# One unit instead of two on plain products, and the order of the first steps, in a fused recurrence-and-MLP kernel

**Chip, cores, metric.** One core of one Trainium2 chip. The metric is the device time of one execution in microseconds (us), median of several executions. The kernel before takes 569.28 us (568.92 to 569.32, three runs). Engine names are those of the profile: PE is TensorE, PEld its weight loads, DVE VectorE, ACT ScalarE, POOL GpSimd.

## The reference

A gated linear recurrence over 768 tokens (4 batches, 8 heads of 48), whose outputs are the 3072 x 384 input of an MLP with an ELU between its two products:

```python
f = 1.0 / (1.0 + np.exp(-f_logit))
for t in range(S):
    state = f[:, :, t, :, None] * state + np.einsum('bhd,bhe->bhde', k[:, :, t], v[:, :, t])
    y[:, :, t] = np.einsum('bhd,bhde->bhe', q[:, :, t], state)
...
h = x @ w_in                                    # 3072x384 @ 384x2048
g = np.where(h > 0.0, h, np.exp(np.minimum(h, 0.0)) - 1.0)
return (g @ w_out).astype(np.float32)           # 3072x2048 @ 2048x384
```

## The kernel before

The 3072 tokens are worked off in twelve **units** of 256. A unit's MLP is eight **pairs**; a pair is one **up** step (part of `x @ w_in`) and, two pairs later, one **down** step (part of `g @ w_out`). Counting ups and downs alike gives steps T0, T1, ...; sixteen belong to a unit. Everything else (attention of the next units, weights, loads) is hung onto steps with `at_step(T, ...)`.

A step has two forms. The *direct* form is plain block products. The *seven-product* form (Strassen-like, 2x2 blocks in seven products) has less PE work and more additions. Units with `m < DIRECT` use the direct form:

```python
DIRECT = 2                      # units 0 and 1 are direct
A1 = (2, 4, 4, 5, 7, 9)         # steps of unit 1's attention; the last three: scores and masks, outputs, carried
D2 = (14, 16, 18, 20); A2 = (22, 24, 24, 26, 27, 28)
MX = 21                         # first mix of the in-weights (POOL)
...
both = (0, 1, 2, 3, 4, 5, 8, 9, 10, 6, 11, 7, 12, 13, 14, 15)    # pairs of units 0 and 1, interleaved
order = [divmod(i, NP) for i in both] + [(m, j) for m in range(2, NU) for j in range(NP)]
...
def down(P):
    m, j = order[P]
    if j == 0:
        pms[m] = [ps.tile([128, DM], FP32, tag=f"m{i + 2 * (m == 1)}", ...) for i in range(NW if m < DIRECT else 4)]
```

The weights arrive as 64-bit numbers in staging slots `area[:, 0..6]`, in sixteen parts, and each part is turned into 32-bit by three steps on two engines: DVE *splits*, ACT *lowers*, DVE *merges*. Seven parts may be under way; a merge frees a slot and fetches the next part:

```python
def split(n):
    nc.vector.tensor_scalar(out=bits[:], in0=hi, scalar1=3, scalar2=0x3FFFFFF8, ...)      # L559
    nc.vector.tensor_scalar(out=hi, in0=hi, scalar1=-(2**30), ...)                        # L563
def lower(n):
    nc.scalar.activation(raw.bitcast(U16)[:, 2::4], raw.bitcast(U32)[:, 0::2], AF.Copy, ...)   # L569
def merge(n):
    nc.vector.tensor_tensor(out=to.bitcast(I32), in0=bits, in1=hi, op=ALU.add)            # L577
    fetch(n + AHEAD)
...
combos = area[:, 0:4]...        # differences of out-weights for the seven products (DVE, `combine`)
mixes = area[:, 4:7]...         # sums of in-weights for the seven products (POOL, `mix`)
...
attention(1, (), A1)
for n in range(1, NFT):
    t = max(needs[n][0] - 2, 0)
    at_step(t, lambda n=n: merge(n))
    if n > 1:
        later.setdefault(max(t - 2, 0), []).append(n)        # split and lower, two steps earlier
at_step(4, lambda: load(2))
at_step(12, lambda: gates(2))
```

## Time and profile before

| | before |
|---|---|
| median of 3 runs | 569.28 us |
| span of the profiled run | 567.4 us |
| first up step, T0 | 29.25 us |
| attention outputs of unit 1 | 51.34 us |
| up step T16 | 77.08 us |
| up step T32 (unit 2 begins) | 124.46 us |
| up step T48 (unit 3 begins) | 168.81 us |

All positions are starts on PE, counted from the beginning of the span, in the timeline of PE. The lines of the page, the chain, the start and the groups are in the prediction below.

### The profile page before, as it was taken

The page shows a single profiled execution, that of the slowest core. Times are in us where ns is not written, and L with a number is a line of the kernel's source. Part 1 is how long each engine was busy: PE and PEld are TensorE (multiplying, and loading weights), DVE is VectorE, ACT ScalarE, POOL GpSimd, SP SyncE. Part 2 cuts the span into 40 slices and gives each one's busy share as a digit, 9 for nine tenths or more (in the row PEclk, how much of TensorE's full clock was granted, in tenths as well). Part 3 has the DMA queues.
Part 4 walks back from the last instruction along what each step waited for, and adds up shares of the span by engine and source line. Part 5 has one row for each costly group of instructions (what it writes and reads, how often), then busy time and mean ns, then how long its engine had stood idle before and what let it go on. Part 6 is the DMA issues. An engine that isn't in the chain of part 4 may idle for free.

```text
span 567.4 us, 15202 instructions
## 1 busy us (share of the span) xinstructions
PE 550.2 (97%) x6226; PEld 501.8 (88%) x6226; DVE 395.2 (70%) x765; ACT 229.3 (40%) x417; POOL 266.3 (47%) x530
## 2 busy tenths in 40 slices
PE   6879999999999999999999999999999999999996
PEld 3457777778999999999999999999999999999995
DVE  8798485835976795885785885786786876745543
ACT  3297737334343443434333343343333343333331
POOL 6510027642374474465366357257257348325332
PEclk9998999999999999999999999999999999999999
DMA  8989780060025125215216216216206203201001
GB/s 207 259 215 297 174 223 14 2 161 29 2 50 140 58 60 143 73 45 152 79 36 155 85 37 154 84 38 154 84 20 172 84 9 72 85 2 36 29 2 35
DMA packets 37902, 53.27 MB, mean 94 GB/s; under 512 B 3680, under 2 KB 27648, under 8 KB 37824
## 3 DMA queue, kind: packets, MB, share of 16 engines
q1 hardware_dynamic: 37024, 51.62, 34.6%
q8 instruction: 51, 0.84, 0.6%
q10 hardware_dynamic: 800, 0.59, 0.5%
q14 instruction: 27, 0.22, 0.1%
HBM read 44.04 MB, written 4.72 MB: 86 GB/s over the span
## 4 chain that ended last, share of the span: by engine, by line
PE 92%; DVE 3%; DMA 2%; issue 1%; ACT 1%; POOL 1%; SPq 0%; DVEq 0%; ACTq 0%; POOLq 0%
PE psH L878 35%; PE psM L977 33%; PE psM L955 8%; PE psH L923 6%; PE psS L701 2%; PE psY L739 2%; PE psY L759 2%; PE psU_a L724 2%; PE psT L665 2%; DMA f<-f 1%; DVE f L627 1%; DMA f<-in_f_logit_dram 1%; ACT area L569 1%; DVE bits L559 0%; PE psY L804 0%
## 5 line engine op out<-in xcount | busy, mean ns | idle before, releaser
L878 PE MATMUL psH<-xt,wi 128*128 128x128 f32 (+1 forms) x960 | 177.1, 293 | 0.0
L942 POOL TENSOR_TENSOR sums<-gg 128x128 f32<-128x128 f32 x160 | 69.5, 455 | 210.8 <-DVE gg L932 202.5
L878 PEld LDWEIGHTS psH<-xt,wi 128*128 128x128 f32 x960 | 135.9, 192 | 0.8
L910 ACT ACTIVATE gg<-hh 128x512 f32<-128x512 f32 x80 | 50.5, 631 | 205.9 <-DVE hh L900 140.5
L878 PE MATMUL psH<-xt,area 128*128 128x128 f32 x640 | 110.5, 275 | 0.0
L878 PEld LDWEIGHTS psH<-xt,area 128*128 128x128 f32 x640 | 96.9, 192 | 4.1
L887 DVE TENSOR_TENSOR hh<-psH,u 128x256 f32<-128x256 f32 x80 | 33.8, 423 | 88.7 <-ACT u L885 88.7
L977 PE MATMUL psM<-area,sums 128*128 128x192 f32 x480 | 91.2, 326 | 0.0
L977 PEld LDWEIGHTS psM<-area,sums 128*128 128x128 f32 x480 | 80.1, 190 | 0.2 <-POOL sums L942 0.2
L977 PE MATMUL psM<-wo,gg 128*128 128x192 f32 x320 | 68.1, 335 | 0.0
L617 POOL TENSOR_TENSOR k<-k,f 128x256 f32<-128x256 f32 x48 | 39.4, 822 | 57.1 <-DMA area<-in_moe_w_in_dram 35.0
L627 DVE RECIPROCAL f<-f 128x256 f32<-128x256 f32 x36 | 62.8, 1747 | 1.3
L911 ACT ACTIVATE gg<-gg 128x512 f32<-128x512 f32 x96 | 60.6, 631 | 3.0
L932 DVE SCALAR_TENSOR_TENSOR gg<-gg,hh 128x512 f32<-128x512 f32 x80 | 55.7, 696 | 1.8 <-ACT gg L911 1.8
L977 PEld LDWEIGHTS psM<-wo,gg 128*128 128x128 f32 x320 | 50.2, 190 | 1.9
L900 DVE TENSOR_TENSOR hh<-psH,u43h 128x256 f32<-128x256 f32 (+1 forms) x160 | 49.8, 353 | 2.7
L923 PE MATMUL psH<-xt,wi 128*128 128x256 f32 x192 | 44.5, 381 | 1.4 <-DVE wi L577 1.2
L942 POOL TENSOR_TENSOR sums<-gg,sums 128x128 f32<-128x128 f32 x80 | 42.8, 535 | 6.3
L955 PE MATMUL psM<-wo,gg 128*128 128x384 f32 x128 | 45.4, 498 | 0.0
L885 ACT COPY u<-psH 128x128 f32<-128x128 f32 x80 | 21.0, 263 | 59.3 <-PE psH L878 59.3
L923 PEld LDWEIGHTS psH<-xt,wi 128*128 128x128 f32 x192 | 35.9, 190 | 8.6 <-issue 1.6
L900 DVE TENSOR_TENSOR u43h<-psH,hh 128x256 f32<-128x256 f32 x80 | 33.9, 423 | 13.4 <-PE psH L878 13.0
(97 smaller groups left out, 721.9 us busy)
## 6 DMA issues: line engine op xcount, KB each, us to landing
area<-in_moe_w_out_dram SPq DMA_DIRECT2D x8, 768.0 KB, 8.9
again<-in_moe_w_in_dram SPq DMA_DIRECT2D x16, 384.0 KB, 4.1
again<-in_moe_w_out_dram SPq DMA_DIRECT2D x16, 384.0 KB, 3.5
k<-in_k_dram SPq DMA_DIRECT2D x12, 384.0 KB, 4.8
q<-in_q_dram SPq DMA_DIRECT2D x12, 384.0 KB, 5.5
v<-in_v_dram SPq DMA_DIRECT2D x12, 384.0 KB, 5.9
area<-in_moe_w_in_dram SPq DMA_DIRECT2D x8, 576.0 KB, 7.2
out_dram<-o SPq DMA_DIRECT2D x38, 96.0 KB, 1.7
```

Source lines behind the costliest of these rows:

```text
L617: e.tensor_tensor(out=t[n][:, p], in0=t[n][:, p], in1=t["f"][:, p, "kq".index(n)], op=ALU.mult)
L627: nc.vector.reciprocal(f[:, p, 1], f[:, p, 0])
L878: nc.tensor.matmul(to, lhsT=lhs, rhs=rhs, start=(n == 0), stop=True, skip_group_check=True)
L887: add = lambda to, x, y: nc.vector.tensor_tensor(out=to, in0=x, in1=y, op=ALU.add)
L900: add = lambda to, x, y: nc.vector.tensor_tensor(out=to, in0=x, in1=y, op=ALU.add)
L910: nc.scalar.activation(g[:], h, AF.Relu, scale=-1.0)
L911: nc.scalar.activation(g[:], g[:], AF.Exp, scale=-1.0)
L923: nc.tensor.matmul(ph[:, i], lhsT=wi[j][:, kt, i * 128 : (i + 1) * 128], rhs=xts[m][:, kt, :], start=(kt == 0), stop=(kt == NKT - 1),)
L932: nc.vector.scalar_tensor_tensor(out=g[:], in0=g[:], scalar=-1.0, in1=phs.pop(P), op0=ALU.add, op1=ALU.max)
L942: nc.gpsimd.tensor_tensor(out=s[:, i], in0=x, in1=y, op=op)
L955: nc.tensor.matmul(pm[t][:], lhsT=g[:, i, t * 128 : (t + 1) * 128], rhs=wo[:, 2 * j + i, :], start=(j == 0 and i == 0), stop=(j == NP - 1 ...
L977: nc.tensor.matmul(pm[bank][:, half * DH : (half + 1) * DH], lhsT=x, rhs=y, start=first, stop=(j == NP - 1), skip_group_check=True,)
```

## The change

The intent: unit 1 too takes the seven-product form, so unit 0 runs its MLP alone while the weights come in, in plain order. The mixes and combinations then have to be ready sooner; they are made in the staging slots as these come free (slots 2 to 4 for the mixes, 5, 6, 0, 1 for the combinations). The first steps are arranged anew: unit 1's state additions at T5, scores at T7, outputs at T8, carried states at T9, and each merge no later than step n.

```diff
-    DIRECT = 2
+    DIRECT = 1
...
-    A1 = (2, 4, 4, 5, 7, 9)
-    D2 = (14, 16, 18, 20)
-    A2 = (22, 24, 24, 26, 27, 28)
+    A1 = (2, 4, 5, 7, 8, 9)
+    D2 = (16, 18, 20, 22)
+    A2 = (23, 25, 25, 26, 27, 28)
...
-    MX = 21
+    MX = 10
+    CB = 16
+    BL1 = 13
...
+        combos = [area[:, i].bitcast(FP32).rearrange("p (n f) -> p n f", f=DH) for i in (5, 6, 0, 1)]
...
-        area[:, 4:7].bitcast(FP32).rearrange("p a f -> p (a f)")[:, 0 : NP * 512]
+        area[:, 2:5].bitcast(FP32).rearrange("p a f -> p (a f)")[:, 0 : NP * 512]
...
-    both = (0, 1, 2, 3, 4, 5, 8, 9, 10, 6, 11, 7, 12, 13, 14, 15)
-    order = [divmod(i, NP) for i in both] + [(m, j) for m in range(2, NU) for j in range(NP)]
+    order = [divmod(i, NP) for i in range(NU * NP)]
...
-            ... tag=f"m{i + 2 * (m == 1)}" ...
+            ... tag=f"m{i + (m < DIRECT)}" ...
...
-        t = max(needs[n][0] - 2, 0)
+        t = min(max(needs[n][0] - 2, 0), n)
...
-    at_step(4, lambda: load(2))
-    at_step(12, lambda: gates(2))
+    at_step(8, lambda: load(2))
+    at_step(14, lambda: gates(2))
...
-        at_step(28 + n, lambda: next(weights))
+        at_step(CB + n, lambda: next(weights))
...
+    at_step(BL1, lambda: blend(1))
```

More of the change, by code (lines that the diff above doesn't have):

```diff
@@ L509, in fast @@
     area = cst.tile([128, AHEAD, 2 * DM], w_in.dtype, name="area") if wide else None
-    combos = cst.tile([128, 4, NP, DH], FP32, name="combos") if not wide else (
-        area[:, 0:4].bitcast(FP32).rearrange("p a f -> p (a f)").rearrange("p (c n f) -> p c n f", c=4, f=DH)
-    )
+    if wide:
+        combos = [area[:, i].bitcast(FP32).rearrange("p (n f) -> p n f", f=DH) for i in (5, 6, 0, 1)]
+    else:
+        apart = cst.tile([128, 4, NP, DH], FP32, name="combos")
+        combos = [apart[:, i] for i in range(4)]
     mixes = cst.tile([128, NP, 4, 128], FP32, name="mixes") if not wide else (
-        area[:, 4:7].bitcast(FP32).rearrange("p a f -> p (a f)")[:, 0 : NP * 512]
+        area[:, 2:5].bitcast(FP32).rearrange("p a f -> p (a f)")[:, 0 : NP * 512]
         .rearrange("p (n c f) -> p n c f", n=NP, c=4)
     )
-    both = (0, 1, 2, 3, 4, 5, 8, 9, 10, 6, 11, 7, 12, 13, 14, 15)
-    order = [divmod(i, NP) for i in both] + [(m, j) for m in range(2, NU) for j in range(NP)]
+    order = [divmod(i, NP) for i in range(NU * NP)]
     needs = sorted(
@@ L840, in combine @@
         b = [[wo[:, i::2, h * DH : (h + 1) * DH] for h in range(2)] for i in range(2)]
-        t = [combos[:, i] for i in range(4)]
+        t = combos
         for n in range(0, NP, 2):
@@ L948, in down @@
         if j == 0:
-            pms[m] = [ps.tile([128, DM], FP32, tag=f"m{i + 2 * (m == 1)}", name=f"psM{m}_{i}") for i in range(NW if m < DIRECT else 4)]
+            pms[m] = [ps.tile([128, DM], FP32, tag=f"m{i + (m < DIRECT)}", name=f"psM{m}_{i}") for i in range(NW if m < DIRECT else 4)]
         pm, g = pms[m], gs.pop(P)
@@ L969, in down @@
         b = [[wo[:, 2 * j + i, h * DH : (h + 1) * DH] for h in range(2)] for i in range(2)]
-        c = [combos[:, i, j] for i in range(4)]
+        c = [combos[i][:, j] for i in range(4)]
         for bank, half, x, y in (
```

## The prediction

> **What bounds the kernel now.** I read the page first: busy shares, then the 40 slices.
>
> ```profile
> PE 550.2 (97%) x6226; PEld 501.8 (88%) x6226; DVE 395.2 (70%) x765; ACT 229.3 (40%) x417; POOL 266.3 (47%) x530
> PE   6879999999999999999999999999999999999996
> DVE  8798485835976795885785885786786876745543
> ```
>
> TensorE (PE) is full from the fifth slice on; only the first four (57 us) have room, and there VectorE (DVE) is nearly full. Next the chain of work that ended last: from 48.8 us on it is PE work almost alone, so PE time saved there is span saved, if nothing else takes its place. It also gives the price of each kind of MLP step (columns: start, us, what).
>
> ```profile
> 43.29 1.72 PE psS L701 x62
> 45.01 3.81 PE psM L955 x8
> 48.82 2.59 PE psH L923 x12
> ...
> 116.88 2.58 PE psM L955 x8
> 119.46 2.59 PE psH L923 x12
> ...
> 164.25 2.44 PE psH L878 x20
> 166.69 2.28 PE psM L977 x14
> ```
>
> A direct pair (six up products L923, four down products L955) takes 2.59 + 2.58 = 5.17 us. A seven-product pair (L878, L977) takes 2.44 + 2.28 = 4.72 us. Then the timeline of PE at the start, and the windows there (after the colon: length; busy us of PE, PEld, DVE, ACT, POOL with counts; clock, DMA share, GB/s).
>
> ```profile
> 37.35 2.83 PE L923 MATMUL psH<-xt,wi 128*128 128x256 f32 x12 [0.19 <-PE psU_a L724]
> 42.78 0.29 PE L701 MATMUL psS<-q,k 64*64 64x64 f32 x2 [2.60 <-issue]
> 43.29 1.72 PE L701 MATMUL psS<-q,k 64*64 64x64 f32 x62 [0.21 <-DVE state L682]
> 44.94 3.88 PE L955 MATMUL psM<-wo,gg 128*128 128x384 f32 x8
> ...
> 44.00:48.00 4.00, 4.00 (x43) 2.59 (x36) 3.90 (x7) 1.93 (x1) 0.00 (x0) 0.62 1.05 251
> ```
>
> PE stands 2.6 us before the scores (L701). They reuse the banks that the four state additions (L682) still read, and DVE reaches these only at 41.4. The clock then drops to 0.62, and the first down step takes 3.81 us, not 2.58. Last the groups, for the weight conversion and the other side work.
>
> ```profile
> L627 DVE RECIPROCAL f<-f 128x256 f32<-128x256 f32 x36 | 62.8, 1747 | 1.3
> L569 ACT ACTIVATE area<-area 128x768 uint16<-128x768 uint32 x16 | 30.4, 1934 | 4.1 <-DVE area L563 3.2 <-DMA q<-in_q_dram 0.8
> L622 DVE TENSOR_TENSOR_SCAN f<-f 128x256 f32<-128x256 f32 x36 | 26.6, 746 | 1.0 <-ACT f L610 1.0
> L577 DVE CUSTOM_DVE_ANT_0 wi<-area,bits 128x1536 uint16<-128x1536 uint16 x8 | 8.0, 1001 | 4.2 <-ACT area L569 3.8 <-ACT between L746 0.4
> L846 DVE TENSOR_TENSOR area<-wo,area 128x384 f32<-128x384 f32 x8 | 5.6, 702 | 0.0
> ```
>
> Each of 16 weight parts costs about 1.15 us of DVE (split, L559 and L563), 1.93 us of ScalarE (ACT, L569), and 1.0 us of DVE (merge, L577).
>
> **What the Trainium skill says.** "Perfetto Trace Analysis", its opening note, calls matmul busy time a bad measure, as matmuls are pipelined. The trace agrees: L878 shows 293 ns for one instruction, but 20 of them take 2.44 us, 122 ns each; so I price steps from the chain. "TensorE: Matmul & The Clock Gate", section "Architectural detail", says ACT and DVE are strict FIFO while PE can pull weight loads ahead. It agrees: unit 0's third up step ended at 40.2, but its activation began at 42.55, behind two L569 passes. Same page, "What's actually happening": the clock halves after an idle window of about 3.4 us. That fits the 0.62 above, after a stretch of 40 to 44 us in which PE was busy 1.19 us. "ScalarE: Activation LUTs", "What ACT_TABLE_LOAD costs", gives 186 + 0.833 N ns for an ACTIVATE with immediates: 613 ns at 512 columns, where the trace has 608 to 631; but 826 at 768, where L569 with its strided 16-bit output takes 1934. The measurement decides, and it makes ACT the engine to watch.
>
> **The change, part by part.** A step T is one up or down step; unit m has steps 16m to 16m+15.
>
> *Unit 1 becomes seven-product.* Eight pairs go from 5.17 to 4.72 us: 8 x 0.45 = 3.6 us less PE, all in the part of the chain that is PE alone. This is sure work removed.
>
> *Side work added for unit 1.* DVE per pair: the additions L887 0.42, L900 0.42 + 0.42 + 0.28, so 1.55 us, 12.4 for eight. POOL: four operations of L942 per pair, some 1.9 to 2.4 us; one more blend of x (five of 0.54 = 2.7 us). ACT: a copy of 0.26 us per pair. Combinations: the same counts, earlier (mixes from T10, combinations T16 to T31).
>
> *The start, reordered.* The scores move from T5 to T7 and the additions to T5, so the first down step need not wait for the scores. Its inputs (activation 35.8, merged weights 39.7) are ready, so it runs 40.2 to 42.8, not 44.9 to 48.7, and with no gap before it I expect no clock loss. The merge of the fourth in-weight stands ahead of the additions now and ends at 42.4, so up step 3 (T6) starts near 42.8 rather than 48.7. Part of these 5.9 us is lent: the scores (1.1 us) come later, and then DVE is the bound. From 41.4 on, per step 2.15 us for a part and 0.34 for half an elu, in order: the additions (2.1) to 45.6, merge and split to 47.6, elu, merge and split to 50.3, masks to 51.5. The attention outputs (T8) wait for these masks, so PE stands about 2.2 us at 49.3. After that PE runs without a gap in my timeline: T8 51.5, T10 58.9, T12 64.1, T14 69.2, T16 at 74.4, against 77.25 before. Gain at T16: 2.8 us.
>
> *ACT in T8 to T15.* It now has six L569 passes (some 1.75 us apart when back to back, 10.5), four activation pairs (4.8), the attention copies with their DMA issue (2.5), and the gates of unit 2 (1.7): 19.5 us in PE's 22.9. It starts behind, and I end the last activation of unit 0 at 75.3, the elu at 75.9, while the second half of the first seven-product step wants its bank at 75.4: a stall of 0.5 us.
>
> *DVE in T16 to T31.* Additions and elus 18 us, decays of units 2 and 3 (six of 0.75 + 1.75) 15, combinations 16 x 0.64 = 10.2, states and masks 2.5: 45.7 us. PE has 16 steps of 2.36 and 5.5 of attention for unit 2: 43.3. So DVE is briefly overbooked, but can carry some lag into T32 and later (a steady unit of 43.74 us has 32.5 of DVE). Going through the orders by hand: about 1.4 us at T22 (the step's additions stand behind the third decay and combination), about 1 at T23 (the transposes need the last scaled k, which waits on a small DMA after that decay, and on POOL), 0.4 at T32 (blend of unit 2). With the 0.5 above: 3.1 us with rounding.
>
> *DMA.* 16 parts of 786 KB. Before, DMA was full from 40 to 62 us and then nearly idle to 68, held by the order of the queue. Unit 2's loads now stand behind all weights. Parts 6 to 15 are 7.9 MB; at the 266 GB/s of 40 to 64 us that takes about 28 us from 38, so the last lands at 64 to 67, and its split in my timeline is at 69: hidden, with 2 us of room.
>
> *Sum.* 3.6 + 2.8 - 3.1 = 3.3 us: 569.3 - 3.3 = 566.0 us.
>
> **Rivals.** (a) *Nothing is lost*: DVE's lag is absorbed. Then 3.6 + 2.8 = 6.4, 562.9 us. For it: the constants of the change look tuned, and before had no stall after 48.8. Against: the DVE count of T16 to T31. (b) *ACT and DVE eat it all*: with L569 in every step to T13, if the elus slip by 2 us more, PE waits at T14 and T16, and DVE starts its overbooked stretch late; in a first, coarser pass I came to unit 2 starting no earlier than before: 569.3 us. For it: ACT waits on DVE's splits and DVE on L569 in turn. Against: ACT had 7 us of waiting for PE in T6 to T16 before. (c) *The DMA becomes the bound*: a split whose part has not landed holds all of DVE behind it, FIFO. If the rate is 230 GB/s the last part lands near 72; 3 us slower than mine: again near 569. For it: the share is over 1.0 from 40 to 62 us. Against: six of the last ten parts are contiguous out-weights, and 48 to 52 us, where such parts moved, had 384 GB/s. (d) A second clock drop at the 2.2 us wait would cost 1 to 1.5 us: 567.3.
>
> **Range and chances.** All runs lie between "nothing lost" and a little worse than "all lost". I put the middle at 566.0, and 8 of 10 between 562.9 and 568.9. Faster by 2% would need 11.2 us, nearly twice everything I can find: 0.01. Slower by 2% would need a wait repeated in every unit; nothing after T48 changes: 0.01. Within 2%: 0.98.
>
> **What would show it right or wrong.** The groups of L923 with 96 and L955 with 64 (halved), L878 with 1760, L977 with 1232 (line numbers move by 3). Right: the first down step near 40 at 2.6 us, clock near 1.0 from 36 to 48, T16 (first L878) near 74.4, unit 2's first L878 near 122, then units of 43.74 us as before. Step by step: a PE wait near 49 on DVE's masks; waits on L900 or on POOL's k between 90 and 98. Wrong: first L878 after 77 (ACT or DMA won: look at what DVE's L559 and the elu L932 wait for), first L878 of unit 2 at or after 124.6, or a unit longer than 43.8 us after it.

## More of the kernel before

Before T0 lies a **head** of about 29 us: the first unit's recurrence, with some idle matmuls (`warm(n)`, each a 128x512 product that nobody reads).

From T48 on nothing is changed, so a stage gained there is gained at the end.

## The result

The changed kernel takes **567.86 us** (567.03 to 568.62, four runs); the kernel before took 569.3 us (568.92 to 570.26) beside it. The ratio is **0.9972**, 95% interval 0.9952 to 0.9992. Ratios here are the mean time of one kernel's fast runs over that of the other's of the same rounds, so not quite the ratio of the medians quoted. By the ratio the gain is 1.6 us (1.4 between the medians), where 3.3 were forecast: about half.

The page of the changed kernel, its busy shares and the slices of PE:

```profile
PE 548.6 (97%) x6338; PEld 510.3 (90%) x6338; DVE 408.2 (72%) x802; ACT 230.6 (41%) x424; POOL 290.9 (51%) x567
PE   6898998999999999999999999999999999999996
```

PE has 1.6 us less to do (550.2 before), DVE 13 us more, POOL 24.6 more. Against the kernel before, the third slice of PE rises from 7 to 9, and the fourth and the seventh fall from 9 to 8: one wait has gone, and small ones have come after it. The timeline of PE says which (start, length, line, operation, and in brackets the wait before it and what ended it; line numbers are 3 higher than before):

```profile
30.80 2.76 PE L926 MATMUL psH<-xt,wi 128*128 128x256 f32 x12
...
41.45 2.74 PE L958 MATMUL psM<-wo,gg 128*128 128x384 f32 x8
44.03 2.75 PE L926 MATMUL psH<-xt,wi 128*128 128x256 f32 x12
...
52.00 0.33 PE L742 MATMUL psY<-at,v 64*64 64x64 f32 x2 [1.35 <-DVE at L712]
52.60 1.16 PE L742 MATMUL psY<-at,v 64*64 64x64 f32 x62 [0.27 <-DVE at L712]
...
60.61 2.75 PE L926 MATMUL psH<-xt,wi 128*128 128x256 f32 x12
...
78.03 0.71 PE L881 MATMUL psH<-xt,area 128*128 128x128 f32 x4 [0.86 <-DVE gg L935]
...
93.85 0.68 PE L881 MATMUL psH<-xt,area 128*128 128x128 f32 x4 [0.49 <-DVE hh L903]
...
97.17 0.44 PE L668 MATMUL psT<-ident,k 128*128 128x128 f32 x2 [0.88 <-POOL k L620]
```

The first down step (L958, 41.45) takes 2.74 us, not 3.88, with no gap before it; up step T6 stands at 44.03, not 48.66. Then PE waits for the masks (L712) at 52.0. From T16 on come the three predicted kinds of stall: 0.86 us for the elu of the first seven-product steps, 0.49 for their additions, 0.88 for POOL's scaled k.

Where the time went, stage by stage. The last column is what the forecast said for the changed kernel; its gain of 2.8 was counted from 77.25, the place of T16 in the chain of the kernel before.

| | before | after | forecast for after |
|---|---|---|---|
| T16 starts | 77.08 | 76.12 (gain 0.96) | 74.4 (gain 2.8) |
| T16 to T32 | 47.38 | 47.60 | 47.6 (T32 "near 122") |
| T32 to T48 | 44.35 | 43.74 | 43.74 |
| T48 to the end of the span | 398.6 | 398.2 | unchanged |

So the stages after T16 came out as forecast, and nearly the whole miss is in the first 76 us: 0.96 us gained there instead of 2.8.

These 76 us have two parts, which meet where unit 1's attention outputs start (L742, when DVE has made the masks). The forecast had the outputs at 51.5 and T16 22.9 us later; measured were 52.00 and 24.12. So of the 1.7 us by which T16 is late, 0.5 lie ahead of the outputs and 1.2 behind them, and these 1.2 all before T10 (8.6 us from the outputs to T10 at 60.61, where the forecast had 7.4).

The clock shows one thing in that stretch. The windows of PE in the kernel before (window, length, PE busy and count, granted clock, DMA share, GB/s), and under them those of the kernel after:

```profile
42.00:44.00 2.00, 1.01 (x39) 0.91 1.05 310
44.00:46.00 2.00, 2.00 (x39) 0.50 1.05 248
46.00:48.00 2.00, 2.00 (x5) 0.74 1.05 255
```
```profile
22.00:26.00 4.00, 2.05 (x98) 1.00 1.07 233
...
26.00:28.00 2.00, 2.00 (x68) 0.58 1.02 309
28.00:30.00 2.00, 2.00 (x20) 0.57 1.06 263
```

The stretch of half clock that stood at the scores of the kernel before (42 to 48) is gone from there, as forecast; another one has appeared at 26 to 30, in the head, whose program is the same in both kernels. It comes after four microseconds in which PE was half idle. T0 is 1.55 us later than before. The theories for the missing 1.9 us of gain (2.8 - 0.96):

- **A, the clock.** A stretch of half clock costs 1 to 2 us wherever it lies (an estimate: at 26 to 30 above, 0.42 and 0.43 of 2 us are lost, 1.7 us in sum). The change takes away one place for it, but it finds another (the head, or the wait for the masks), so the gain booked for it is not had.
- **B, the chain of weight parts.** DVE and ACT convert the parts, and this chain alone fixes when T8 and T16 can start; the clock only goes along.
- **C, the side work.** The earlier mixes and combinations slow DVE and POOL, or the seven products for unit 1 give back more than they save.
- **D, the transfers.** The parts land later than DVE could take them.

### The profile page after: what moved, and what is told of

Same layout as the page of the kernel before. It is cut to its first block, busy times and chain, and to the rows that moved or that the text cites. A ratio compares the mean times of both kernels' runs of the same rounds, so it can differ in the third digit from the quotient of the medians.

```text
span 565.7 us, 15532 instructions
## 1 busy us (share of the span) xinstructions
PE 548.6 (97%) x6338; PEld 510.3 (90%) x6338; DVE 408.2 (72%) x802; ACT 230.6 (41%) x424; POOL 290.9 (51%) x567
## 4 chain that ended last, share of the span: by engine, by line
PE 82%; DVE 6%; ACT 4%; DMA 4%; issue 2%; POOL 1%; SPq 0%; ACTq 0%; DVEq 0%; POOLq 0%
PE psH L881 37%; PE psM L980 36%; DMA area<-in_moe_w_in_dram 2%; ACT area L572 2%; PE psS L704 2%; PE psY L742 2%; PE psY L762 2%; PE psU_a L727 2%; DVE f L630 2%; PE psT L668 1%; DMA f<-f 1%; DVE f L625 1%; DVE bits L562 1%; DMA f<-in_f_logit_dram 0%; DVE area L566 0%
## 5 line engine op out<-in xcount | busy, mean ns | idle before, releaser
L881 PE MATMUL psH<-xt,wi 128*128 128x128 f32 (+1 forms) x1056 | 194.9, 293 | 0.0
L945 POOL TENSOR_TENSOR sums<-gg 128x128 f32<-128x128 f32 x176 | 77.5, 461 | 216.3 <-DVE gg L935 204.9
L881 PEld LDWEIGHTS psH<-xt,wi 128*128 128x128 f32 x1056 | 149.5, 192 | 1.4
L881 PE MATMUL psH<-xt,area 128*128 128x128 f32 x704 | 121.8, 275 | 1.4 <-DVE gg L935 0.9
L881 PEld LDWEIGHTS psH<-xt,area 128*128 128x128 f32 x704 | 106.5, 191 | 6.4 <-DVE gg L935 1.0
L980 PE MATMUL psM<-area,sums 128*128 128x192 f32 x528 | 100.3, 326 | 0.0
L980 PEld LDWEIGHTS psM<-area,sums 128*128 128x128 f32 x528 | 88.2, 190 | 0.1
L980 PE MATMUL psM<-area,gg 128*128 128x192 f32 x176 | 43.0, 326 | 0.0
L980 PE MATMUL psM<-wo,sums 128*128 128x192 f32 x176 | 43.0, 326 | 0.0
L945 POOL TENSOR_TENSOR sums<-sums,gg 128x128 f32<-128x128 f32 x88 | 42.8, 487 | 0.0
```

Source lines behind the costliest of these rows:

```text
L881: nc.tensor.matmul(to, lhsT=lhs, rhs=rhs, start=(n == 0), stop=True, skip_group_check=True)
L945: nc.gpsimd.tensor_tensor(out=s[:, i], in0=x, in1=y, op=op)
L980: nc.tensor.matmul(pm[bank][:, half * DH : (half + 1) * DH], lhsT=x, rhs=y, start=first, stop=(j == NP - 1), skip_group_check=True,)
```

## The experiments

Fifteen runs in four batches, each in the same rounds with the kernel before. The times first; each is a median with its range.

| run | us | ratio to before, 95% interval |
|---|---|---|
| before, again | 568.74 (567.93 to 569.48) | 0.9994 [0.9968, 1.0019] |
| after, again | 567.38 (566.76 to 567.95) | 0.9971 [0.9947, 0.9995] |
| after, a third time | 567.97 (565.95 to 569.35) | 0.9982 [0.9953, 1.0011] |
| more warming in the head | 567.27 (566.91 to 568.0) | 0.9973 [0.995, 0.9996] |
| gates one step later | 567.44 (566.1 to 568.78) | 0.9982 [0.9956, 1.0007] |
| seven products off | 568.23 (567.53 to 569.55) | 0.9991 [0.9956, 1.0026] |
| old start in the new kernel | 568.6 (567.53 to 569.65) | 0.9983 [0.9947, 1.002] |
| new start in the old kernel | 571.38 (568.43 to 572.2) | 1.0021 [0.9979, 1.0063] |
| mixes later | 575.11 (574.3 to 576.9) | 1.0109 [1.007, 1.0148] |
| masks first | 567.85 (567.61 to 568.36) | 0.9983 [0.9957, 1.0009] |
| side work of T16 on rearranged | 567.3 (564.74 to 567.54) | 0.9974 [0.9949, 1.0] |
| both of these | 566.68 (565.99 to 569.1) | 0.9969 [0.9941, 0.9997] |
| after, waits filled | 566.69 (566.19 to 566.91) | 0.9952 [0.9933, 0.9971] |
| rearranged, waits filled | 565.63 (564.3 to 567.48) | 0.9932 [0.9911, 0.9954] |
| before, wait filled | 568.4 (567.82 to 569.22) | 0.9985 [0.9964, 1.0005] |

The differences are small beside the spread of single runs, so the stage positions in the profiles carry the argument and the times check it. These are the positions in the ten profiles in which the new start runs in the plain order, with DVE's masks left where the change puts them (us; "stretch" is where 2-us windows between 14 and 78 us show a clock below full):

| profile | stretch | T0 | outputs | outputs to T16 | T16 |
|---|---|---|---|---|---|
| after | 26 to 30 | 30.80 | 52.00 | 24.12 | 76.12 |
| after, again | 18 to 24 | 30.73 | 52.31 | 24.12 | 76.43 |
| after, a third time | 52 to 56 | 28.78 | 51.48 | 25.35 | 76.83 |
| seven products off | 18 to 24 | 30.07 | 51.77 | 24.11 | 75.88 |
| mixes later | 52 to 56 | 28.13 | 50.95 | 25.39 | 76.34 |
| more warming in the head | none | 30.16 | 51.82 | 24.11 | 75.93 |
| gates one step later | none | 28.81 | 51.34 | 24.12 | 75.46 |
| side work rearranged | none | 28.20 | 50.45 | 24.11 | 74.56 |
| after, waits filled | none | 28.73 | 50.78 | 24.11 | 74.89 |
| rearranged, waits filled | none | 28.91 | 52.25 | 24.11 | 76.36 |
| forecast | none | | 51.5 | 22.9 | 74.4 |

Three things can be read from it. From the outputs to T16 it takes 24.1 us in every profile without a stretch there, so 1.2 us of the miss have nothing to do with the clock. A stretch behind the outputs adds 1.2 to 1.3 us. And the start of the outputs scatters between 50.45 and 52.25 even where the clock is whole: T16 is at 75.4 on average there and at 76.3 with a stretch, 0.9 us apart, but the two groups overlap.

**1. The same kernels again.** No edit.

> The kernel before, unchanged, to see how much a second profile differs. Theory H (the missing gain lies ahead of the first up step, in a stretch where both programs are the same and the granted clock falls or not by chance): the first up step starts anywhere from 29.2 to 31 us, and the dip of the clock may lie at 26 to 30 or at 43 to 47 us. Rival S (the stage from the first seven-product step on was mis-sized, the head is a property of each program): first up step again at 29.2 to 29.4, dip again at 43 to 47. Time 569 to 570 under both.

> The changed kernel, unchanged. Theory H: the first up step is not again at 30.8 without fail; if it is at 29.3 in this profile, the profiled span is about 1.5 us shorter (564.2). From the first up step to the first seven-product step 45.3 us, from there to the first step of unit 2 47.8, both within 0.3 of the first profile. Rival S: first up step again at 30.8 and the clock again at one half from 26 to 29.5. Time 567 to 568.6.

> The changed kernel once more on this chip, with five rounds. First up step between 28.7 and 31 us as the dip of the clock falls; first seven-product step 75.4 to 76.5; unit 2 47.6 us later; time 567 to 568, 0.9965 to 0.998 of the kernel before. If the forecast of 566.0 was right after all and the first measurements were unlucky: 565.7 to 566.5.

The kernel before repeats its start closely: T0 at 28.73 (below the 29.2 of both expectations), T16 at 77.14, half clock at 44 to 48, the place that rival S had named. The kernel after doesn't repeat the *place* of its slow stretch, though T0 was late again in the second profile (30.73). It lay at 18 to 24 in the second profile (T16 at 76.43) and at 52 to 56 in the third (T16 at 76.83). In the third, T0 was at 28.78, as in the kernel before, and the loss came behind the wait for the masks; the timeline of PE and the windows there:

```profile
51.48 0.32 PE L742 MATMUL psY<-at,v 64*64 64x64 f32 x2 [1.60 <-DVE at L712]
52.08 1.82 PE L742 MATMUL psY<-at,v 64*64 64x64 f32 x62 [0.27 <-DVE at L712]
53.84 3.77 PE L926 MATMUL psH<-xt,wi 128*128 128x256 f32 x12
```
```profile
52.00:54.00 2.00, 1.92 (x63) 0.58 1.03 239
54.00:56.00 2.00, 2.00 (x6) 0.57 1.05 326
```

The same 62 matmuls that took 1.16 us in the first profile take 1.82, and the up step after them 3.77 instead of 2.86. (T16 at 76.83 lies above the 75.4 to 76.5 expected for this run.) All three profiles of the changed kernel have a slow stretch, in three places; each loses 1.7 us in the sum of its windows, as much as 3.4 us at half clock. (In the second, the head also stood 2.24 us for POOL's k at 18.05, so not all of its late T0 is clock.)

**2. More warming in the head.** Two idle matmuls between the merge of part 0 and the second half of the first outputs.

```diff
     merge(0)
+    warm(2, "m3")
     first_outputs(1)
```

> The changed kernel with two more idle products on the tensor engine between the two parts of unit 0's outputs, where it waits for a copy. Theory H: the clock stays at 1.00 from 20 to 30 us, the first up step starts at 29.2 to 29.8 and the median falls by 0.8 to 1.5 us against the changed kernel (566.4 to 567). Rival S: the head does not matter for the end; within 0.3 us of the changed kernel.

Measured: no window below full clock, T0 at 30.16, T16 at 75.93, 567.27 us, the same as the unfilled kernel (567.38) in these rounds; neither the T0 (29.2 to 29.8) nor the time (566.4 to 567) of theory H came. The clock stayed up, but these matmuls stand in PE's queue at a place where it waits only 0.46 us and cost 1.9 us themselves, so T0 came nearly as late as with the slow stretch. Inconclusive as a cure: other profiles have a whole clock without it, and a filling that lies outside a wait costs its own length.

**3. Gates of unit 2 one step later.**

```diff
-    at_step(14, lambda: gates(2))
+    at_step(15, lambda: gates(2))
```

> The changed kernel with the two gate passes of unit 2 on the scalar engine one step later, behind the last activation of unit 0. If the scalar engine's order makes the wait of 0.86 us in the first seven-product step: that wait goes, the scan of unit 2 starts at most 0.6 us earlier or at the same time, and from the first seven-product step to unit 2 it takes 46.9 to 47.3 us instead of 47.8; time 0.5 to 1 us less. If another wait takes its place (the vector engine is booked without a gap from 77 to 98 us): the stage stays at 47.5 to 47.8 and the time is the same.

Measured: 567.44 us, the same, where 0.5 to 1 us less was expected. But its profile (a run of 566.1 us) happens to have no slow stretch at all: T0 28.81, T16 **75.46**. That is still 1.06 us later than the forecast 74.4, so the clock can't be the whole miss. T16 to T32 took 46.69 instead of 47.60: the wait of 0.86 us for the elu at the first seven-product step is gone, as ACT is no longer held by the gates. So that stall was what the prediction took it for; it was worth 0.9 us in this stage, where 0.5 was priced.

**4. Seven products off for unit 1,** with all else as in the changed kernel.

```diff
-    DIRECT = 1
+    DIRECT = 2
...
-    at_step(BL1, lambda: blend(1))
```

> The changed kernel with unit 1 back to direct products (one unit after the other, same start, same early combinations). If the seven products are worth what the chain of the kernel before says (5.17 against 4.72 us for a pair): from the first up step of unit 1 to unit 2 it takes 46.8 to 47.4 us, with no wait for the vector engine's additions, and the two down steps that fall behind it are 0.3 us longer each. The changed kernel took 47.60 there with 2.2 us of waits, so the seven products would have bought nearly nothing in that stage: time within 0.6 us of the changed kernel (567 to 568.4). If they are worth 3.6 us after all: 2 us or more slower than the changed kernel (569.5 and over).

Measured: T16 at 75.88, T16 to T32 47.38, T32 to T48 44.34; 568.23 us. In T16 to T48 the direct unit 1 takes 91.72 us, the seven-product unit 1 91.34. So the 3.6 us of PE work saved are worth 0.4 us net (0.4 to 0.8 with the other two profiles of the changed kernel); the rest is waits. The prediction's sum for these (3.6 - 3.1 = 0.5) holds. Theory C in its second form is true, but it was forecast and is not the miss.

**5. Old start in the new kernel, new start in the old.**

```diff
# old start in the new kernel
-    A1 = (2, 4, 5, 7, 8, 9)
+    A1 = (2, 4, 4, 5, 7, 9)
# new start in the kernel before
-    A1 = (2, 4, 4, 5, 7, 9)
+    A1 = (2, 4, 5, 7, 8, 9)
```

> The changed kernel with unit 1's attention at the steps of the kernel before. If the order of the start is what gains: the wait of 2.6 us ahead of the scores is back, the first seven-product step starts at 77 to 78 us, not 76.1, and the time is 568.5 to 570. If weights for unit 0 alone bound the start in any order: first seven-product step at 76 to 76.5, time 567 to 568.

> The kernel before with only the steps of unit 1's attention as in the change (state additions one step, scores two steps later). If the start's gain comes from this order: the first down step follows the third up step at 40 us without a gap, the clock stays at 1.00 from 40 to 48 us, and unit 2 starts 1.5 to 2.5 us earlier than the 124.46 of the kernel before (122 to 123); time 567 to 567.8, as good as the whole change. If it comes from unit 0 alone: no earlier than 124.2, time 569.

Measured: with the old start in the new kernel the 2.6 us wait before the scores is back at 42.73, the slow stretch is back at 42 to 50, and T16 is at 78.35: 2.2 us later than with the new start. Not all of this is the order: the profiled run was the slowest of this kernel, and its slow stretch is twice as long (its windows lose 3.4 us, not 1.7). With the new start in the old kernel the wait for the scores is gone, but T12 waits 1.95 us for a transfer of x and T16 is at 80.3 (two slow stretches, 26 to 32 and 54 to 58): no gain, 571.38 us (this too is the profile of its slowest run, 572.2). So the new start alone isn't the gain; that it needs the plain order of unit 0's pairs, where unit 1's attention isn't needed before T16, is argued and was not tried apart. Also, a head with a slow stretch is no property of the changed kernel: here the old kernel with the new start has one.

**6. Mixes four steps later.**

```diff
-    MX = 10
+    MX = 14
```

> The changed kernel with GpSimd's weight mixtures four steps later. In the changed kernel the weight splits on the vector engine take 0.70 us in place of 0.56 and the merges 1.15 to 1.20 in place of 0.95 from 61 to 73 us, the time in which GpSimd makes the mixtures. If the two engines slow each other: splits at 0.56 and merges at 0.95 there, the last merge 0.5 to 1 us earlier, and the slowed instructions then lie later (scans, additions). If it is something else (the weights' arrival): splits stay at 0.70. Time within 0.7 us of the changed kernel either way.

Measured: 575.11 us, 1.1% slower, where at most 0.7 us was expected. The reason is one line of PE's timeline:

```profile
102.96 0.69 PE L668 MATMUL psT<-ident,k 128*128 128x128 f32 x2 [6.67 <-POOL k L620]
```

The mixes that now come later stand in POOL's queue ahead of the scaling of k for unit 2, and PE stands 6.67 us before the transposes. It is the wait of 0.88 us of the changed kernel, enlarged, and the clock is 0.50 to 0.54 from 100 to 106, around its end. The run shows one more thing: DVE's splits took 0.56 us and its merges 0.96 up to 67 us, then 0.70 and 1.21, from about the moment POOL began to work (a blend of x at 67.76, mixes from 72.11). In the changed kernel the mixes begin sooner. The groups of DVE between 68 and 76 us, first of the kernel before, with POOL busy for 0.72 of the 8 us, then of the kernel after, with POOL busy for 7.68 (after the bar: busy us, mean ns):

```profile
L577 DVE CUSTOM_DVE_ANT_0 wo<-area,bits 128x1536 uint16<-128x1536 uint16 x1 | 1.0, 959 | 1.3 <-ACT area L569 1.3
L563 DVE TENSOR_SCALAR area<-area 128x768 int32<-128x768 int32 x1 | 0.6, 563 | 0.0
```
```profile
L580 DVE CUSTOM_DVE_ANT_0 wo<-area,bits 128x1536 uint16<-128x1536 uint16 x3 | 3.4, 1148 | 0.5 <-ACT area L572 0.5
L566 DVE TENSOR_SCALAR area<-area 128x768 int32<-128x768 int32 x2 | 1.4, 700 | 0.1
```

This is theory C in its first form, real in the durations. But PE runs from T10 to T16 without a wait, so it is hidden until the first seven-product steps.

**7. Masks first.** The masks of unit 1 go ahead of the merge of part 6 in DVE's queue. The merge moves one step later, and the split of part 8 with it, as only two buffers hold split parts.

```diff
-        t = min(max(needs[n][0] - 2, 0), n)
+        t = min(max(needs[n][0] - 2, 0), n) + (n == 6)
...
-            later.setdefault(max(t - 2, 0), []).append(n)
+            later.setdefault(max(t - 2 - (n == 6) + (n == 8), 0), []).append(n)
```

> The changed kernel with the masks of unit 1's scores ahead of one weight merge and one split on the vector engine (these follow it). If the masks' place in that queue is what eats the start's gain between the fourth and the sixth up step: outputs start 1 to 1.5 us earlier against the first up step, and the first seven-product step starts at 74.8 to 75.4 us where the clock does not dip (76.1 and 76.4 in the two profiles of the changed kernel, 75.5 in one without a dip). If the weights' conversion behind it is the bound (vector and scalar engine in turn): the wait only moves to a later up or down step, and the first seven-product step stays at 75.5 to 76.4.

Measured: the outputs start at 50.07 instead of 51.48 to 52.31, without a wait. But T10 starts at 62.33 and T16 at 77.84. The gain turned into another wait, in PE's timeline:

```profile
56.78 1.93 PE L762 MATMUL psY<-q,state 64*64 64x64 f32 x64 [1.93 <-ACT between L749]
```

The small copies of ACT (L749) that the carried product needs stand behind the lowering of a part, and this was delayed with the merge. So near T8 there is no room in the chain of DVE and ACT: theory B holds that far. The profile has a slow stretch as well, at 56 to 62, around this new wait.

**8. Side work from T16 on rearranged, alone and with the masks first.** Gates at T15, the combinations spread over T16 to T32 away from the crowded steps, and POOL's scaling of the last k put first.

```diff
-        scale(u, ("q", NKT - 1, nc.gpsimd), ("k", NKT, nc.gpsimd), ("q", NKT, nc.gpsimd))
+        scale(u, ("k", NKT, nc.gpsimd), ("q", NKT - 1, nc.gpsimd), ("q", NKT, nc.gpsimd))
...
-    at_step(14, lambda: gates(2))
+    at_step(15, lambda: gates(2))
...
-        at_step(CB + n, lambda: next(weights))
+        at_step((16, 17, 18, 19, 22, 23, 24, 24, 26, 27, 28, 28, 30, 31, 32, 32)[n], lambda: next(weights))
```

> The changed kernel with three moves in the stage from the first seven-product step to unit 2: unit 2's gates one step later, the combinations of the out weights thinned around the third decay of unit 2 (none in two steps, two in later ones), and the last scaled k ahead of a scaled q on GpSimd. If the waits there are what keeps the seven products from paying: that stage takes 45.4 to 46.2 us instead of 47.60, the waits of 0.86, 0.49 and 0.88 us shrink to under 0.5 in sum; time 1.2 to 2 us less than the changed kernel. If something else binds: 46.7 or more, as with the gates alone.

> Both of the former together. If the two gains add: unit 2 starts at 120.5 to 121.5 us, time 565 to 566, that is 0.993 of the kernel before. If they do not: 566.5 to 567.5.

Measured: T16 to T32 45.72 us alone and 45.20 with the masks first, against 47.23 to 47.60 in the changed kernel; T32 to T48 0.43 us longer. So in these two profiles 1.1 to 2 us of the stalls after T16 are gone. The profiled run of the first was its fastest, 564.74 us, with no slow stretch (T16 at 74.56); its other runs went up to 567.54. The time of the first, 0.7 us under the changed kernel's in these rounds, missed the 1.2 to 2 us expected. Both edits together, 566.68 us with unit 2 at 122.13, had a slow stretch at 56 to 60; by the expectation the two gains don't add. The gain of the stage is visible in the profiles and drowned in the times by the scatter of the start. This made the start's scatter the question.

**9. The waits filled.** If theory A is right, idle matmuls *inside* the waits must hold the clock, cost nothing, and bring T16 and the time down. In the kernels after: one 128x512 matmul where the head waits (in the first outputs, before the padded products), one ahead of the outputs of unit 1. In the kernel before: two, in the wait before its scores.

```diff
# after, and the rearranged kernel
         for gap in range(2):
+            if gap and not part:
+                warm(1)
...
+    at_step(A1[4], lambda: warm(1))
     attention(1, (), A1)
# before
+    at_step(A1[3], lambda: warm(2, "m3"))
     attention(1, (), A1)
```

> The changed kernel with two idle matmul fillings (one 128x512 matmul each, some 0.9 us of TensorE): one in the head where the profile shows a wait of 1.05 to 1.34 us in L807, one just before the attention outputs of unit 1 (L742), where it waits 1.35 to 1.6 us for the masks. Theory A (the missing part of the forecast start is the half-clock stretch, which falls now in the head, now after the mask wait): clock 1.00 in every 2-us window from 16 to 62 us, first up step at 28.2 to 28.9, T16 at 75.2 to 75.6 (75.5 was seen in the one undisturbed profile of nearly the same program), time 566.3 to 566.9, with a smaller spread of runs than the 566.0 to 569.4 of the unfilled kernel. Theory B (the clock is no cause: VectorE's and ScalarE's chain of weight parts sets T16): T16 at 76.1 to 76.8 as before and a time of 567.4 to 568.0, or slower by the fillings.

> The same two fillings in the kernel whose combinations and scales of unit 2 stand in another order (c_stage_only, 567.3 in median, but 564.74 in its undisturbed profiled run). Theory A: clock 1.00 throughout 16 to 62 us, T16 at 74.6 to 75.5, T16 to T32 45.7, median 565.0 to 565.8. Theory B: the median stays at 567 to 567.5, and 564.74 was luck of another kind.

> The kernel before, with two idle matmuls (some 1.9 us) in its 2.6 us wait ahead of the scores of unit 1. Theory A: the clock stays 1.00 from 40 to 48 us, the 62 scores take 1.15 us rather than 1.72, the first down step 2.75 rather than 3.88, T6 at 47.0 to 47.3 rather than 48.7, T16 at 75.5 to 75.9, time 567.4 to 568.2: then about 1.3 us of what I booked as gained by the new start is to be had without it. Theory B: the step after the scores waits for something else instead, T16 stays at 77.1 and the time at 569.

Measured, **after filled**: full clock in every window from 16 to 62 us, and T16 at **74.89**. The windows and the timeline of PE:

```profile
22.00:26.00 4.00, 3.57 (x130) 1.00 1.10 229
...
16.00:62.00 46.00, 42.56 (x624) 1.00 0.99 246
```
```profile
48.80 1.02 PE L1037 MATMUL psW<-ident 128*128 128x512 f32 x2
50.78 0.33 PE L742 MATMUL psY<-at,v 64*64 64x64 f32 x2 [0.95 <-DVE at L712]
51.38 1.16 PE L742 MATMUL psY<-at,v 64*64 64x64 f32 x62 [0.28 <-DVE at L712]
...
59.38 2.75 PE L928 MATMUL psH<-xt,wi 128*128 128x256 f32 x12
...
74.89 0.38 PE L883 MATMUL psH<-xt,wi 128*128 128x128 f32 x2
```

T16 is even 0.3 us earlier than theory A had said, and the time is the one it said. The six runs lie within 0.72 us, against 1.2 to 3.4 us for the same kernel unfilled, and the ratio to before goes from 0.9971 to 0.9982 (three measurements without filling) to 0.9952. The intervals of these ratios overlap, and the kernel before was slower and more scattered on this chip (569.89 in median, 568.04 to 571.16), so the times speak for the filling without proving it. Nor does this profile refute theory B: from the outputs to T16 it has the same 24.11 us as the others, and it gains on them by outputs that start earlier (50.78); the other kernel filled in this way, below, does not repeat that.

**Before filled**: full clock from 40 to 48 us.

```profile
42.84 1.16 PE L701 MATMUL psS<-q,k 64*64 64x64 f32 x62 [0.21 <-DVE state L682]
43.93 2.85 PE L955 MATMUL psM<-wo,gg 128*128 128x384 f32 x8
...
65.73 2.83 PE L923 MATMUL psH<-xt,wi 128*128 128x256 f32 x12 [0.87 <-ACT area L569]
```

The scores take 1.16 us and the first down step 2.85, as expected, and T6 stands 2.05 us earlier (46.61). Half of that is given back at 65.73, where T12 now waits 0.87 us for ACT, so T16 is at 76.14: 0.94 us earlier than without the filling, where 1.2 to 1.6 were expected. The time, 568.4 us, has a ratio of 0.9985, whose interval still holds 1.

**Rearranged and filled**: full clock from 16 to 62, and at 565.63 us (0.9932) the fastest kernel in median; its interval lies wholly below 1, and 4.3 us of medians lie between it and the kernel before. The expected median (565.0 to 565.8) came. The expected T16 (74.6 to 75.5) did not, nor did the 45.7 us from T16 to T32 (46.94): the profiled run was its slowest, 567.48 us, with T16 at 76.36, which is where theory B had put it. This can't be the clock, and DVE's timeline names it:

```profile
42.97 0.56 DVE L562 TENSOR_SCALAR bits<-area 128x768 int32<-128x768 int32 x1 [0.91 <-DMA area<-in_moe_w_in_dram]
...
50.44 0.56 DVE L562 TENSOR_SCALAR bits<-area 128x768 int32<-128x768 int32 x1 [0.72 <-DMA area<-in_moe_w_in_dram]
```

Two splits waited 1.6 us together for their parts to land, and the masks behind them came 1.5 us later than in the other filled kernel (outputs at 52.25 instead of 50.78). So theory D is true as a second source of scatter, as large as the slow stretch, once PE and DVE are in time. In the first profile of the changed kernel, with its late head, no split waited for a part at all; in the third, with T0 at 28.78, one did, 1.02 us. That would explain why a head that is 2 us late costs less than 2 us at the outputs, as DVE then finds parts landed for which it would have waited; no run tested it. The fillings did nothing for the scatter of this kernel (3.2 us, and 2.8 without them).

## Why the prediction was wrong

- **What bounds the kernel** was right: PE, with the start as the only place with room and DVE and ACT nearly full there.
- **Seven products for unit 1, 3.6 us less PE**: right in size where nothing waits (pairs of 4.7 us against 5.17, or 5.0 while the down step is still a direct one of unit 0).
- **The stalls that take it back, 3.1 us**: right in sum, uneven in the parts. For T16 to T32 the forecast was 47.6 us and the three profiles have 47.23 to 47.60. The elu stall was 0.79 to 0.86 us, not 0.5; the additions cost 0.49, not 1.4; POOL's k 0.78 to 0.88, as the 1 us said; the wait at T32 didn't show. The rest went into slower first pairs. (The four parts as written, 0.5 + 1.4 + 1 + 0.4, sum to 3.3 and not to 3.1.)
- **The start, 2.8 us: this is the step that failed, in two places.** The larger one is the overlap: "After that PE runs without a gap in my timeline: T8 51.5, T10 58.9". Measured were 8.6 us from the outputs to T10, not 7.4, in each of the eight profiles of the table without a slow stretch there. Against the same four pieces in the kernel before (1.09, 2.68, 1.09 and 2.69, so 7.55 us from their starts on PE), 0.60 go into the outputs, which stop once more for the second part of the masks (0.27 us, after two products that take 0.33 alone), and 0.46 into the carried product, whose first weight load waits 0.50 us for an ACT copy that stands behind a lowering; the last 0.15 is the forecast's smaller prices of the pieces. So DVE and ACT still set PE's pace there; the run with the masks first shows it from the other side, as the wait moved from the outputs to the carried product and grew.
- The other place is "with no gap before it I expect no clock loss". That was true of the down step: clock 1.00 at 36 to 48, 2.74 us. But all three profiles of the changed kernel have a slow stretch elsewhere. In the third it lies behind the outputs and costs 1.24 us, which is the prediction's rival (d), "a second clock drop", at the place and the size that it named. In the other two it lies in the head, where nobody looked for it, and the outputs come 0.5 and 0.8 us later than forecast. So T16 is late by 1.7, 2.0 and 2.4 us: 1.2 from the overlap each time, the rest at most from the clock. That rival (d) also came near to the time, 567.3 us, is in part luck, as it knew nothing of the 1.2.
- **The filled kernel's T16 of 74.89, near to the forecast, is in part luck too**: its outputs start at 50.78, 0.7 us earlier than forecast, and this hides over half of the 1.2 us behind them. The other profiles with a whole clock have T16 at 74.56 to 76.36.
- **What of the new start is then left?** Filled against filled, it gains 76.14 - 74.89 = 1.25 us in one profile each. Another 0.94 us is to be had in the kernel before by two idle matmuls alone.
- **The transfers** were rightly held to be hidden in the first profile; with a faster start they are the next to show. (7.9 MB at 266 GB/s are 29.6 us, not 28, so the forecast had some 1.4 us of room and not 2.)
- **In numbers of the whole**: filled against filled, the change is worth 568.4 - 566.69 = 1.7 us of medians: 1.25 at T16, -0.1 from T16 to T32, 0.6 from T32 to T48.

What stays open: what a slow stretch in the head costs at T16, as the profiles with and without one overlap, and whether it is more frequent in the changed kernel than in the one before. The program is the same up to T0; the profiles of the kernel before had none there, the version with the new start had one. These profiles are too few to say. The filling of the head and that of the mask wait were not tried apart, and no run takes away the 1.2 us behind the outputs without putting another wait in their place. And the filled kernels ran in another batch and on another chip than the unfilled ones, so they are compared through the kernel before.

## What to carry to other kernels

A wait taken away uncovers the next one: follow the other engines' queues through the steps behind it before writing "without a gap", for here the second half of the masks and one small copy cost 1.1 us in every profile. A gain that comes from taking away a stretch of slow clock can be lost again if another half-idle stretch is left nearby: price the start with and without it. Where a wait can't be removed, matmuls that nobody reads can be tried in it, inside the wait and shorter than it; the one run that placed them outside paid 1.9 us for them. When the profile of one run and the median of many disagree, take two more profiles of the same kernel before explaining anything.

## What the Trainium skill lacked or had wrong

- "TensorE: Matmul & The Clock Gate", section "What's actually happening", speaks of an idle window of about 3.4 us before the clock halves. Here it halved after four microseconds with 2.05 us of work (22 to 26 in the first profile of the changed kernel), and didn't after others with 2.13 us (48 to 52, with the gates later, and in the rearranged kernel). So being half idle was enough in one place and not in another, and the page gives no share of work that keeps the clock up. Its free-running window agrees with what was seen: one program had its slow stretch at 26 to 30, 18 to 24 and 52 to 56. It calls the ramp penalty below 1% of a typical span. That agrees (1.7 us of 567 is 0.3%), and yet it is as much as the whole change brings.
- No page was found to say whether idle matmuls inside a wait steady a kernel's time. The changed kernel had a range of 0.7 us with them (six runs) and of 1.2 to 3.4 us without (four to six); the rearranged kernel had 3.2 us with them and 2.8 without, where late transfers scatter it.
- "GPSIMD Engine Reference", section "Specifications", says that GpSimd shares its SBUF interfaces with VectorE and names the kinds of instruction that contend; that section gives no size. Here, with POOL at work, splits (one SBUF input) went from 0.56 to 0.70 us and merges (two inputs) from 0.96 to between 1.15 and 1.21.
- "ScalarE: Activation LUTs", section "What ACT_TABLE_LOAD costs": its formula gives 826 ns at 768 columns; the lowering, with 16-bit outputs at a stride, took 1934. The page has no term for such an output.
